# Hedgehog attention beside a Mish FFN on one core: transposes by DMA, the v copy on ScalarE, a new load order and warm-up matmuls

## The chip, the cores and the metric

The kernel runs on one core of a Trainium2 chip. The metric is the device time of one execution in microseconds (us). Below, PE is TensorE (matmuls), PEld its weight loads, DVE is VectorE, ACT is ScalarE, POOL is GpSimd, and SP is SyncE, which here only issues DMA transfers. "Granted clock" is the TensorE clock that the profile reports, as a share of full speed. "Cold" below means that matmuls take as long as the first six v matmuls of the kernel before, 2.29 us (382 ns each), and "warm" that they take as long as its later ones, 1.30 us (217 ns each).

## The reference, cut to what matters

```python
x  = A_x                                  # 1 x 2048 x 448, bf16
xn = layernorm(x)
# linear attention, 16 heads of 28 columns
q, k, v = split_heads(xn @ wqkv)
pq, pk  = q @ w_phi, k @ w_phi            # per head, 28 x 28
phi     = concat(softmax(p), softmax(-p)) # for q and for k
o       = (phi_q @ (phi_k^T v)) / (phi_q @ sum(phi_k) + 1e-6)
# FFN, 448 -> 1792 -> 448, h * tanh(softplus(h)) is Mish
h       = xn @ w1 + b1
out     = x + o @ wo + mish(h) @ w2
```

The kernel multiplies w_phi into the q and k weights first (the products are called Wp), so that one matmul gives pq or pk. For that it transposes the q and k weights; and its matmuls that contract over the 448 columns read xn transposed (the tile xnT).

## The kernel before

Rows are taken in 8 pairs of 128-row tiles; j counts pairs. The operations are recorded by a helper that adds the waits and keeps one list per engine, in the order of the code. One pass of the projection loop, for one pair, is called an iteration; "xT of pair 7" is the transposed xn of pair 7. These are the parts that matter; cuts are marked.

```python
# start-up
dma("SP", x_all[:, 0:2, :], ...)
wload("ACT", Wqkv[:, :, D:2 * D], A_wqkv[:, D:2 * D], "Wk")
dma("SP", x_all[:, 2:4, :], ...)
wload("SP", Wqkv[:, :, 2 * D:3 * D], ..., "Wv")
# ... x 4 to 7, Wq, x 8 to 15, W1, W2, Wo, all on SP
for j in range(4):                         # block-diagonal w_phi
    dma("ACT", Wbd[DH * j:DH * (j + 1), :, DH * j:DH * (j + 1)], ..., r=["Wbd"], w=[f"Wbd{j}"])

def w_trans(which, h):                     # weights transposed on PE, then copied by ACT
    b = 4 + h                              # the banks of the k matmuls
    # ... 8 x e.transpose(PSb[0:KP, b, ...], Wqkv[:, c, col:col + KP], ident[:])
    act(lambda a: a.activation(WT[...], PSb[0:KP, b, :]..., ACT.Copy), ...)

def w_mm(which, h):                        # weights times Wbd, banks 6 and 7, copied by ACT
    # ... 8 matmuls
    act(lambda a: a.activation(Wp[:, which, 2 * h:2 * h + 2, :], PS[:, 6:8, 0:D], ACT.Copy), ...)

def xT(j):                                 # xn transposed on PE, then copied by ACT
    for u in range(2):
        pe(lambda e, t=t, u=u: transp(e, b, xn[t % NXN], u), ...)
    act(lambda a: a.activation(xnT[:, :, 256 * j:256 * j + 256], PSb[:, b, :]..., ACT.Copy), ...)

def vevac(j):                              # v copied out of PSUM by DVE
    dve(lambda v: v.tensor_copy(v_ext[:, 2 * j:2 * j + 2, :, 0:DH], PS[:, 2:4, 0:D]...), ...)

for j in range(NP):                        # the projection loop, NP = 8
    if j + 3 < NP:
        ln_a(j + 3)                        # DVE statistics, POOL rstd
    if j + 1 < NP:
        xT(j + 1)
    if j == 1:
        w_mm(0, 0); w_mm(0, 1)             # q weights
    proj(j, j - 1 if j else None)          # PE: v(j), q(j-1), k(j); vevac(j); q exponentials on ACT
    kexp(j)                                # ACT: two exponentials of k
    if j == 0:
        w_trans(0, 0); w_trans(0, 1)       # q weights
    if j + 2 < NP:
        ln_b(j + 2)                        # DVE: xn of two tiles
    if j >= 2:
        knorm(j - 2)                       # DVE: sum, reciprocal; POOL: product phik
# ... then the FFN with the attention's second half between, and the output
```

The softmax here doesn't subtract the row's maximum and nothing guards it: scores larger than these inputs give would overflow.

## Time and profile before

| | before |
|---|---|
| median of the runs | 186.0 us |
| span of the profiled execution | 184.0 us |
| first v matmul | 12.40 us |
| v matmuls of pair 1 / pair 2 / pair 7 start | 23.11 / 28.11 / 58.01 us |
| last k matmul of the loop ends | 62.55 us |
| first Mish starts | 68.77 us |

From the first Mish on PE is busy for 48.77 of the first 49.20 us, so the table cuts the kernel in three: start-up, loop, FFN. The page of the profile shows the first two in the 40 slices, each 4.6 us long; a digit is the busy share in tenths.

```profile
PE   0775599679879999999999999999999999999993
DVE  1576035989898891148888888300121121121211
ACT  1763749775696884445667666875000000000000
```

PE has its holes in the first five slices, and small ones up to the twelfth. There (slices 8 to 12) DVE is at 8 and 9 while PE is at 6 to 9. An average over the whole span would hide both.

The chain of waits (start, duration, what), followed back from the last instruction, is this in the start-up:

```profile
3.34 5.44 DMA Wbd<-in_A_w_phi_dram
8.91 0.92 PE PS L294 x8
9.85 0.93 ACT Wp L298
...
12.61 2.09 PE PS L309 x6
...
16.46 1.73 ACT hm L358 x2
18.33 0.64 PE PS L284 x8
18.99 1.94 ACT hm L287 x2
20.93 0.91 ACT xnT L321
21.84 0.82 ACT Wp L298
22.70 0.57 PE PS L294 x8
```

Here L294 is the product of weights and w_phi, L298 its copy, L358 the exponentials of k, L284 and L287 the q weight transposes and their copies. Between the k matmuls of pair 0 (16.4 us) and the v matmuls of pair 1 (23.1 us), PE has only 0.64 and 0.57 us of the chain, and ACT nearly all the rest. (PE is busy for 2.49 of these 6.69 us in all; ACT for 5.39.) The transposes of the q weights even wait for the exponentials of k, since they use the same PSUM banks.

The timeline of one iteration of the loop (start, duration, engine, line, operation, output and input, shape, count; in brackets the idle time before it and what ended it):

```profile
46.85 0.70 PE L304 MATMUL PS<-ident,xn 128*128 128x128 bf16 x8 [1.17 <-DVE xn L273]
47.03 2.00 DVE L364 TENSOR_REDUCE Sk<-hm 128x64 f32<-128x1792 bf16 x1
47.39 1.30 PE L309 MATMUL PS<-Wqkv,xnT 128*128 128x448 bf16 x6
...
49.07 0.55 DVE L366 RECIPROCAL rSk<-Sk 128x64 f32<-128x64 f32 x1
49.70 3.21 POOL L367 TENSOR_TENSOR hm<-hm,rSk 128x1792 bf16<-128x1792 bf16 x1 [2.03 <-DVE rSk L366]
...
50.32 1.09 DVE L504 CAST v_ext<-PS 128x896 bf16<-128x896 f32 x1 [0.70 <-PE PS L314]
...
51.33 2.02 DVE L273 TENSOR_SCALAR xn<-x_all,mv,rstd 128x448 bf16<-128x448 bf16 x2
...
53.10 0.70 PE L304 MATMUL PS<-ident,xn 128*128 128x128 bf16 x8 [1.17 <-DVE xn L273]
```

Read it as a ring: PE transposes xn and multiplies; the v copy on DVE waits for PE; xn comes behind the v copy on DVE; PE waits for xn. From 46.85 to 53.10 us the ring takes 6.25 us. The two xn take 2.02 us here, where they start under POOL's product (49.70 to 52.91 us), and 0.69 us where POOL is idle (at 27.13 and 32.05 us). The first of the two takes 1.71 us and ends at 53.04 us, 0.13 us after the product; "held by POOL" below means this.

### The profile page before, as it was taken

The numbers are of one execution on the slowest core, as the hardware profiler recorded it, in microseconds if no ns is written. First come the engines' busy times: TensorE is split into PE (matmuls) and PEld (weight loads), VectorE is DVE, ScalarE is ACT, GpSimd is POOL, SyncE is SP. The second block draws the span as 40 slices with busy tenths as digits, with TensorE's granted clock in tenths as the row PEclk, the third lists the DMA queues.
The fourth block names the chain that finished last, engine by engine and source line by source line (L and its number), as shares of the span: only waits on it lengthen the run. The fifth ranks groups of instructions, "written<-read, shape, count | busy, mean of one in ns | idle before, by whom it ended". The sixth has DMA issues, their size and how long they took to land.

```text
span 184.0 us, 2742 instructions
## 1 busy us (share of the span) xinstructions
PE 164.6 (89%) x1143; PEld 86.5 (47%) x1153; DVE 90.1 (49%) x172; ACT 84.6 (46%) x86; POOL 51.8 (28%) x54
## 2 busy tenths in 40 slices
PE   0775599679879999999999999999999999999993
PEld 0551445334444476645555555434445445445441
DVE  1576035989898891148888888300121121121211
ACT  1763749775696884445667666875000000000000
POOL 4340102395546699104444444200000000000000
PEclk9999999999999999999999999999999999999999
DMA  6999800000000000000000000000001001001001
GB/s 177 349 405 368 258 0 0 0 2 4 0 0 0 2 4 0 4 0 0 4 0 0 4 0 0 0 4 0 25 25 50 28 26 50 27 25 53 25 25 50
DMA packets 7957, 9.15 MB, mean 50 GB/s; under 512 B 1033, under 2 KB 7177, under 8 KB 7945
## 3 DMA queue, kind: packets, MB, share of 16 engines
q1 hardware_dynamic: 6864, 8.49, 13.6%
q10 hardware_dynamic: 1048, 0.48, 0.9%
q8 instruction: 9, 0.15, 0.4%
q14 instruction: 4, 0.02, 0.0%
q0 software_dynamic: 32, 0.00, 0.0%
HBM read 7.14 MB, written 1.84 MB: 49 GB/s over the span
## 4 chain that ended last, share of the span: by engine, by line
PE 81%; DVE 9%; ACT 3%; DMA 3%; issue 1%; ACTq 1%; POOL 0%; POOLq 0%; DVEq 0%
PE PS L309 37%; PE PS L477 23%; PE PS L314 7%; PE PS L410 4%; PE PS L384 4%; PE PS L304 4%; DVE xn L273 3%; DMA Wbd<-in_A_w_phi_dram 3%; DVE v_ext L504 2%; DVE Sk L364 2%; PE PS L294 1%; ACT hm L287 1%; ACT Wp L298 1%; ACT hm L358 1%; ACTq L169 1%
## 5 line engine op out<-in xcount | busy, mean ns | idle before, releaser
L477 PE MATMUL PS<-W,hm 128*128 128x448 bf16 x224 | 43.8, 352 | 0.0
L309 PE MATMUL PS<-xnT,W 128*128 128x512 bf16 x158 | 41.2, 379 | 0.5
L464 ACT ACTIVATE hm<-PS,b1T 128x1024 bf16<-128x1024 f32 x28 | 31.2, 1115 | 20.4 <-PE PS L314 11.6
L488 DVE TENSOR_TENSOR out_sb<-PS,x_all 128x448 bf16<-128x448 f32 x16 | 10.0, 624 | 55.2 <-PE PS L314 33.5
L477 PEld LDWEIGHTS PS<-W,hm 128*128 128x128 bf16 x224 | 21.9, 98 | 20.5
L367 POOL TENSOR_TENSOR hm<-hm,rSk 128x1792 bf16<-128x1792 bf16 x8 | 25.6, 3213 | 14.4 <-DVE rSk L366 9.2
L375 ACT ACTIVATE EqT<-PS 112x1024 bf16<-112x1024 f32 x16 | 15.5, 1021 | 11.9 <-PE PS L314 11.9
L309 PEld LDWEIGHTS PS<-xnT,W 128*128 128x128 bf16 x168 | 14.5, 97 | 11.6 <-issue 1.2
L504 DVE CAST v_ext<-PS 128x896 bf16<-128x896 f32 x8 | 8.7, 1090 | 15.7 <-PE PS L314 15.7
L364 DVE TENSOR_REDUCE Sk<-hm 128x64 f32<-128x1792 bf16 x8 | 16.0, 1995 | 0.0
L358 ACT ACTIVATE hm<-PS 128x896 bf16<-128x896 f32 x16 | 13.8, 925 | 2.8 <-PE PS L309 2.8
L410 PEld LDWEIGHTS PS<-KVZ,EqT 112*128 112x128 bf16 x128 | 9.0, 97 | 9.1 <-DVE t_0 L424 3.0
L309 PE MATMUL PS<-Wqkv,xnT 128*128 128x448 bf16 x48 | 11.6, 378 | 1.5 <-DVE b1T L549 1.5
L427 POOL TENSOR_TENSOR o_sb<-t_0,rden 128x448 bf16<-128x448 f32 x8 | 7.5, 943 | 17.4 <-DVE rden L426 17.4
L410 PE MATMUL PS<-KVZ,EqT 112*128 112x120 bf16 x128 | 12.1, 216 | 0.0
L309 PE MATMUL PS<-Wo,EqT 128*128 128x448 bf16 x48 | 11.8, 354 | 0.0
L309 PE MATMUL PS<-xnT,Wp 128*112 128x512 bf16 x48 | 11.7, 380 | 0.0
L261 DVE BATCH_NORM_STATS2 stats<-x_all 128x6 f32<-128x448 bf16 x16 | 9.1, 610 | 3.8 <-DMA x_all<-in_A_x_dram 3.8
L427 POOL TENSOR_TENSOR o_sb<-t_1,rden 128x448 bf16<-128x448 f32 x8 | 7.5, 942 | 11.1 <-DVE rden L426 11.1
L309 PE MATMUL PS<-Wp,xnT 128*128 128x448 bf16 x48 | 10.5, 354 | 0.0
L273 DVE TENSOR_SCALAR xn<-x_all,mv,rstd 128x448 bf16<-128x448 bf16 x16 | 9.3, 619 | 2.3 <-POOL rstd L269 2.3
L304 PE MATMUL PS<-ident,xn 128*128 128x128 bf16 x64 | 6.2, 244 | 3.6 <-DVE xn L273 3.6
(59 smaller groups left out, 162.3 us busy)
## 6 DMA issues: line engine op xcount, KB each, us to landing
W<-in_B_w_dram SPq DMA_DIRECT2D x2, 896.0 KB, 10.5
out_dram<-out_sb SPq DMA_DIRECT2D x16, 112.0 KB, 1.7
W<-in_B_w_dram SPq DMA_DIRECT2D x1, 1568.0 KB, 15.6
Wqkv<-in_A_wqkv_dram SPq DMA_DIRECT2D x4, 224.0 KB, 5.6
x_all<-in_A_x_dram SPq DMA_DIRECT2D x1, 896.0 KB, 7.9
Wqkv<-in_A_wqkv_dram ACTq DMA_DIRECT2D x2, 224.0 KB, 4.0
x_all<-in_A_x_dram SPq DMA_DIRECT2D x2, 224.0 KB, 3.4
x_all<-in_A_x_dram SPq DMA_DIRECT2D x1, 448.0 KB, 5.9
```

What stands on the lines that cost most here:

```text
L273: eng(lambda v: v.tensor_scalar(xn[t % NXN][:, :], x_all[:, t, :], mv[:, t, 0:1], rstd[:, t:t + 1], op0=ALU.subtract, op1=ALU.mult), r=[f" ...
L304: i = e.transpose(PSb[:, bank, o:o + P], src[:, C0[c]:C0[c] + P], ident[:])
L309: i = e.matmul(out, lhs[:, c, :], rhs[:, c, :], start=(start and n == 0), stop=(stop and n == 2))
L314: return e.matmul(out, lhs[h, 1 + u, :], rhs[h, 1 + u, :], start=start, stop=stop)
L358: act(lambda a, s=s: a.activation(Ek[j % 4][:, :, s, :], PS[:, 4:6, 0:D], ACT.Exp, scale=(1.0 if s == 0 else -1.0)), w=[f"Ek{j % 4}{s}"], ...
L364: dve(lambda v: v.tensor_reduce(Sk[b][:, :], Ek[q][:, :, :, :].rearrange("p t s (h f) -> p (t s h) f", f=DH), AX.X, ALU.add), r=[f"Ek{q}0" ...
L367: pool(lambda g: g.tensor_tensor(phik[:, 2 * j:2 * j + 2, :].rearrange("p t (k f) -> p (t k) f", f=DH), Ek[q][:, :, :, :].rearrange("p t s ...
L375: act(lambda a, s=s: a.activation(EqT[0:KP, s, 2 * gp:2 * gp + 2, tc * 512:(tc + 1) * 512], PS[0:KP, 6:8, :], ACT.Exp, scale=(1.0 if s == ...
L410: i = e.matmul(PS[:, b, g * QG * E2:(g + 1) * QG * E2], EqT[0:KP, s, g, t * P:(t + 1) * P], KVZ[:, s, g, :, :], start=True, stop=True)
L427: pool(lambda g: g.tensor_tensor(o_sb[t % NO][:, :].rearrange("p (h d) -> p h d", d=DH), t1[i][:, :, 0:DH], ap_on(rden[i][:, 0:1], [[1, H] ...
L464: act(lambda a: a.activation(hm[tcp][:, fc, :].rearrange("p (u n) -> p u n", u=2), PS[:, b:b + 2, :], ACT.Mish, bias=b1T[:, fc:fc + 1]), r ...
L477: i = e.matmul(PS[:, bs[u], 0:D], hm[t // 8][:, fc, o:o + P], W2[:, fc, :], start=(u == 0 and fc == 0), stop=(u == 1 and fc == FC - 1))
```

## The change

Its intent: take transposes and their copies off PE and ACT, take the v copy off DVE, shorten the way to Wbd, and have PE at full clock when real work begins.

The new x layout writes xn with its overlapping column chunks already side by side (512 instead of 448 columns), so that one DMA transpose takes a whole pair. The diff, cut to its core (all cuts marked with `# ...`):

```diff
+    def dma_t(eng, out, in_, r=(), w=()):
+        return pr.add(eng, lambda e: e.dma_start_transpose(out, in_), r=r, w=w, dma=True)
-    xnT = sb("xnT", [P, KC, S])
+    xnT = sb("xnT", [P, NT, KC, P])
# ...
-    wload("SP", Wqkv[:, :, 0:D], A_wqkv[:, 0:D], "Wq")
-    dma("SP", x_all[:, 8:16, :], xv[:, 8:16, :], w=[f"x{t}" for t in range(8, 16)])
-    wload("SP", W1[:], B_w1, "W1")
-    dma("SP", W2[:], B_w2.rearrange("(c p) d -> p c d", p=P), w=["W2"])
-    wload("SP", Wo[:], A_wo, "Wo")
+    for g in range(QG):
+        dma_t("SP", WTq[:, g:g + 1, :], A_wqkv[:, g * KP:g * KP + P], w=[f"WTq{g}"])
+    dma("ACT", x_all[:, 8:16, :], xv[:, 8:16, :], w=[f"x{t}" for t in range(8, 16)])
# ... four Wbd loads become one load of w_phi and a masked product on POOL
+    pool(lambda g: g.tensor_tensor(Wbd[:]..., ap_on(wraw[...]), ap_on(mask[...]), ALU.mult), ...)
# ... ln_norm writes 512 columns; w_trans remains for the k weights only
-        act(lambda a: a.activation(Wp[:, which, 2 * h:2 * h + 2, :], PS[:, 6:8, 0:D], ACT.Copy),
-            w=[f"Wp{which}"], x=[6, 7])
+        if eng is act:
+            act(lambda a: a.activation(out, src, ACT.Copy), w=[f"Wp{which}{h}"], x=[bs, bs + 1])
+        else:
+            eng(lambda v: v.tensor_copy(out, src), w=[f"Wp{which}{h}"], x=[bs, bs + 1])
# ...
     def xT(j):
         b = j % 2
+        src = xn[j % NXN]
+        if j >= 2:
+            dma_t("SP", xnT[:, 2 * j:2 * j + 2, :, :].rearrange("p t c n -> p (t c) n"),
+                  src[:].rearrange("p t n -> p (t n)"), r=[...], w=[f"xT{j}"])
+            return
# ... pairs 0 and 1 stay on PE and ACT
     def vevac(j):
-        dve(lambda v: v.tensor_copy(v_ext[:, 2 * j:2 * j + 2, :, 0:DH],
+        act(lambda a: a.activation(v_ext[:, 2 * j:2 * j + 2, :, 0:DH],
# ...
+    pe(lambda e: [e.matmul(PS[:, 7, 0:P], ident[:], ident[:], start=True, stop=True) for _ in range(NWARM)][-1],
+       r=["ident"], x=[7])                 # NWARM = 48, ahead of everything on PE
# ...
     for j in range(NP):
+        if j == 1:
+            w_mm(0, 0, 6, act)
+            w_mm(0, 1, 0, dve)
# ...
         if j + 2 < NP:
             ln_b(j + 2)
+            xT(j + 2)
+            if j < 2:
+                wload("SP", W1[:], B_w1, "W1", (j,))
+            elif j == 4:
+                dma("SP", W2[:], B_w2.rearrange("(c p) d -> p c d", p=P), w=["W2"])
+            elif j == 5:
+                wload("SP", Wo[:], A_wo, "Wo")
```

More of the change, by code (lines that the diff above doesn't have):

```diff
@@ L175, in _kernel @@
     Wbd = sb("Wbd", [KP, QG, KP])
+    wraw = sb("wraw", [KP, QG, DH])
     mask = sb("mask", [KP, QG, E1], FP32)
@@ L179, in _kernel @@
     x_all = sb("x_all", [P, NT, D])
-    xnT = sb("xnT", [P, KC, S])
-    Wqkv = sb("Wqkv", [P, KC, 3 * D])
+    xnT = sb("xnT", [P, NT, KC, P])
+    Wk = sb("Wk", [P, KC, D])
+    Wv = sb("Wv", [P, KC, D])
     Wp = sb("Wp", [P, 2, KC, D])
@@ L189, in _kernel @@
     mhalf = sb("mhalf", [P, 4], FP32)
-    NXN = 6
-    xn = [sb(f"xn{i}", [P, D]) for i in range(NXN)]
+    NXN = 3
+    xn = [sb(f"xn{i}", [P, 2, KC * P]) for i in range(NXN)]
     Sk = [sb(f"Sk{i}", [P, 4 * H], FP32) for i in range(2)]
@@ L200, in _kernel @@
     Ek = [hm0[:, EK0 + i * 4 * D:EK0 + (i + 1) * 4 * D].rearrange("p (t s f) -> p t s f", t=2, s=2) for i in range(4)]
-    WT = hm0[0:KP, 0:2 * KC * QG * P].rearrange("p (w c g n) -> p w c g n", w=2, c=KC, g=QG)
+    WTk = hm0[0:KP, 0:KC * QG * P].rearrange("p (c g n) -> p c g n", c=KC, g=QG)
+    WTq = hm0[:, KC * QG * P:KC * QG * P + QG * D].rearrange("p (g n) -> p g n", g=QG)
     phik = hm[1].rearrange("p a b -> p (a b)").rearrange("p (t f) -> p t f", t=NT)
@@ L218, in _kernel, with wload @@
     FULL = ((0, 2, 3), (0, 1, 3))
-    def wload(eng, dst, src, key):
-        for h in range(2):
+    def wload(eng, dst, src, key, hs=(0, 1)):
+        for h in hs:
             dma(eng, dst[:, 2 * h:2 * h + 2, :],
@@ L228, in _kernel @@
     dma("SP", x_all[:, 0:2, :], xv[:, 0:2, :], w=["x0", "x1"])
-    wload("ACT", Wqkv[:, :, D:2 * D], A_wqkv[:, D:2 * D], "Wk")
+    dma("ACT", wraw[:], bass.AP(tensor=A_w_phi.tensor, offset=A_w_phi.offset, ap=[[DH, KP], [4 * DH * DH, QG], [1, DH]]), w=["wraw"])
+    wload("ACT", Wk[:], A_wqkv[:, D:2 * D], "Wk")
     dma("SP", x_all[:, 2:4, :], xv[:, 2:4, :], w=["x2", "x3"])
-    wload("SP", Wqkv[:, :, 2 * D:3 * D], A_wqkv[:, 2 * D:3 * D], "Wv")
+    wload("SP", Wv[:], A_wqkv[:, 2 * D:3 * D], "Wv")
@@ L239, in _kernel @@
     pool(lambda g: g.memset(ident[:], 0.0), w=["ident"])
-    pool(lambda g: g.memset(Wbd[:], 0.0), w=["Wbd"])
     pool(lambda g: g.memset(mhalf[:], -0.5), w=["mhalf"])
+    pool(lambda g: g.memset(mask[:], 1.0), w=["mask"])
     pool(lambda g: g.affine_select(out=ident[:], in_=ident[:], compare_op=ALU.not_equal, fill=1.0, base=0,
                                    pattern=[[-1, P]], channel_multiplier=1), r=["ident"], w=["ident"])
-    for j in range(4):
-        dma("ACT", Wbd[DH * j:DH * (j + 1), :, DH * j:DH * (j + 1)],
-            A_w_phi.rearrange("(g j) d f -> j d g f", j=4)[j], r=["Wbd"], w=[f"Wbd{j}"])
+    for base, cm, st in ((0, 1, -DH), (DH - 1, -1, DH)):
+        pool(lambda g, base=base, cm=cm, st=st: g.affine_select(
+            out=mask[:], in_=mask[:], compare_op=ALU.is_ge, fill=0.0, base=base,
+            pattern=[[st, QG], [0, E1]], channel_multiplier=cm), r=["mask"], w=["mask"])
@@ L247, in _kernel @@
     dma("POOL", b1_rows[:], B_b1.rearrange("(c p) -> c p", p=P), w=["b1r"])
+    pool(lambda g: g.tensor_tensor(Wbd[:].rearrange("p g (j f) -> p g j f", f=DH),
+                                   ap_on(wraw[:, 0, 0:1], [[DH, QG], [0, QG], [1, DH]]),
+                                   ap_on(mask[:, 0, 0:1], [[0, QG], [E1, QG], [1, DH]]), ALU.mult),
+         r=["wraw", "mask"], w=["Wbd"])
     def masks():
-        pool(lambda g: g.memset(mask[:], 1.0), w=["mask"])
-        for base, cm, st in ((0, 1, -DH), (DH - 1, -1, DH)):
-            pool(lambda g, base=base, cm=cm, st=st: g.affine_select(
-                out=mask[:], in_=mask[:], compare_op=ALU.is_ge, fill=0.0, base=base,
-                pattern=[[st, QG], [0, E1]], channel_multiplier=cm), r=["mask"], w=["mask"])
@@ L272, in ln_norm, with w_trans @@
     def ln_norm(t, eng):
-        eng(lambda v: v.tensor_scalar(xn[t % NXN][:, :], x_all[:, t, :], mv[:, t, 0:1], rstd[:, t:t + 1],
+        i = (t // 2) % NXN
+        eng(lambda v: v.tensor_scalar(xn[i][:, t % 2, :].rearrange("p (a b) -> p a b", a=2),
+                                      ap_on(x_all[:, t, 0:1], [[192, 2], [1, 256]]), mv[:, t, 0:1], rstd[:, t:t + 1],
                                       op0=ALU.subtract, op1=ALU.mult),
-            r=[f"x{t}", f"mv{t}", f"rs{t}"], w=[f"xn{t % NXN}"])
-    def w_trans(which, h):
+            r=[f"x{t}", f"mv{t}", f"rs{t}"], w=[f"xn{i}{t % 2}"])
+    def w_trans(h):
         b = 4 + h
@@ L281, in f, with w_mm @@
                 for g in range(QG):
-                    col = which * D + g * KP
                     o = ((c % 2) * QG + g) * P
-                    i = e.transpose(PSb[0:KP, b, o:o + P], Wqkv[:, c, col:col + KP], ident[:])
+                    i = e.transpose(PSb[0:KP, b, o:o + P], Wk[:, c, g * KP:(g + 1) * KP], ident[:])
             return i
-        pe(f, r=[("Wk" if which else "Wq") + str(h), "ident"], x=[b])
-        act(lambda a: a.activation(WT[:, which, 2 * h:2 * h + 2, :, :], PSb[0:KP, b, :].rearrange(
-            "p (c g n) -> p c g n", c=2, g=QG), ACT.Copy), w=[f"WT{which}{h}"], x=[b])
-    def w_mm(which, h):
+        pe(f, r=[f"Wk{h}", "ident"], x=[b])
+        act(lambda a: a.activation(WTk[:, 2 * h:2 * h + 2, :, :], PSb[0:KP, b, :].rearrange(
+            "p (c g n) -> p c g n", c=2, g=QG), ACT.Copy), w=[f"WTk{h}"], x=[b])
+    def w_mm(which, h, bs, eng):
         def f(e):
@@ L293, in f @@
                 for g in range(QG):
-                    i = e.matmul(PS[:, 6 + c % 2, g * KP:(g + 1) * KP], WT[:, which, c, g, :],
+                    lhs = WTk[:, c, g, :] if which else WTq[0:KP, g, C0[c]:C0[c] + P]
+                    i = e.matmul(PS[:, bs + c % 2, g * KP:(g + 1) * KP], lhs,
                                  Wbd[:, g, :], start=True, stop=True)
             return i
-        pe(f, r=[f"WT{which}{h}"] + [f"Wbd{j}" for j in range(4)], x=[6, 7])
-        act(lambda a: a.activation(Wp[:, which, 2 * h:2 * h + 2, :], PS[:, 6:8, 0:D], ACT.Copy),
-            w=[f"Wp{which}"], x=[6, 7])
+        pe(f, r=([f"WTk{h}"] if which else [f"WTq{g}" for g in range(QG)]) + ["Wbd"], x=[bs, bs + 1])
+        out, src = Wp[:, which, 2 * h:2 * h + 2, :], PS[:, bs:bs + 2, 0:D]
+        if eng is act:
+            act(lambda a: a.activation(out, src, ACT.Copy), w=[f"Wp{which}{h}"], x=[bs, bs + 1])
+        else:
+            eng(lambda v: v.tensor_copy(out, src), w=[f"Wp{which}{h}"], x=[bs, bs + 1])
     def transp(e, bank, src, u):
@@ L305, in transp @@
         return i
+    ALLP = slice(0, P)
     def full(e, out, lhs, rhs, u, start=True, stop=False):
         for n, c in enumerate(FULL[u]):
-            i = e.matmul(out, lhs[:, c, :], rhs[:, c, :], start=(start and n == 0), stop=(stop and n == 2))
+            i = e.matmul(out, lhs(ALLP, c), rhs(ALLP, c), start=(start and n == 0), stop=(stop and n == 2))
         return i
@@ L313, in rem, with f, xs, sl @@
         h = slice(HP * u, HP * (u + 1))
-        return e.matmul(out, lhs[h, 1 + u, :], rhs[h, 1 + u, :], start=start, stop=stop)
+        return e.matmul(out, lhs(h, 1 + u), rhs(h, 1 + u), start=start, stop=stop)
     def xT(j):
         b = j % 2
-        for u in range(2):
-            t = 2 * j + u
-            pe(lambda e, t=t, u=u: transp(e, b, xn[t % NXN], u), r=[f"xn{t % NXN}", "ident"], x=[b])
-        act(lambda a: a.activation(xnT[:, :, 256 * j:256 * j + 256],
-                                   PSb[:, b, :].rearrange("p (c n) -> p c n", c=KC), ACT.Copy),
-            w=[f"xT{j}"], x=[b])
+        src = xn[j % NXN]
+        if j >= 2:
+            dma_t("SP", xnT[:, 2 * j:2 * j + 2, :, :].rearrange("p t c n -> p (t c) n"),
+                  src[:].rearrange("p t n -> p (t n)"), r=[f"xn{j % NXN}{u}" for u in range(2)], w=[f"xT{j}"])
+            return
+        for u in range(2):
+            def f(e, u=u):
+                for c in range(KC):
+                    o = (u * KC + c) * P
+                    i = e.transpose(PSb[:, b, o:o + P], src[:, u, c * P:(c + 1) * P], ident[:])
+                return i
+            pe(f, r=[f"xn{j % NXN}{u}", "ident"], x=[b])
+        act(lambda a: a.activation(xnT[:, 2 * j:2 * j + 2, :, :].rearrange("p t c n -> p (t c n)"),
+                                   PSb[:, b, :], ACT.Copy), w=[f"xT{j}"], x=[b])
+    def xs(t, n):
+        if n == 1:
+            return lambda h, c: xnT[h, t, c, :]
+        return lambda h, c: xnT[h, t:t + n, c, :]
+    def sl(w):
+        return lambda h, c: w[h, c, :]
     def vargs(j, u):
         t = 2 * j + u
-        return PS[:, 2 + u, 0:D], xnT[:, :, t * P:(t + 1) * P], Wqkv[:, :, 2 * D:3 * D]
+        return PS[:, 2 + u, 0:D], xs(t, 1), sl(Wv)
     def kargs(j, u):
         t = 2 * j + u
-        return PS[:, 4 + u, 0:D], xnT[:, :, t * P:(t + 1) * P], Wp[:, 1, :, :]
+        return PS[:, 4 + u, 0:D], xs(t, 1), sl(Wp[:, 1, :, :])
     def qargs(i, u):
@@ L335, in qargs @@
         g = 2 * gp + u
-        return PS[0:KP, 6 + u, :], Wp[:, 0, :, g * KP:(g + 1) * KP], xnT[:, :, tc * 512:(tc + 1) * 512]
+        return PS[0:KP, 6 + u, :], sl(Wp[:, 0, :, g * KP:(g + 1) * KP]), xs(4 * tc, 4)
     def proj(j, i):
@@ L343, in proj @@
                 pe(lambda e, u=u: full(e, *qargs(i, u), u),
-                   r=[f"xT{2 * (i // 2)}", f"xT{2 * (i // 2) + 1}", "Wp0"], x=[6 + u])
+                   r=[f"xT{2 * (i // 2)}", f"xT{2 * (i // 2) + 1}", "Wp00", "Wp01"], x=[6 + u])
         pe(lambda e: (rem(e, *vargs(j, 0), 0), rem(e, *vargs(j, 1), 1))[1], x=[2, 3])
@@ L349, in proj @@
         pe(lambda e: (rem(e, *kargs(j, 0), 0, True, False), rem(e, *kargs(j, 1), 1, True, False))[1],
-           r=["Wp1"], x=[4, 5])
+           r=["Wp10", "Wp11"], x=[4, 5])
         if i is not None:
@@ L353, in proj @@
         for u in range(2):
-            pe(lambda e, u=u: full(e, *kargs(j, u), u, False, True), r=[f"xT{j}", "Wp1"], x=[4 + u])
+            pe(lambda e, u=u: full(e, *kargs(j, u), u, False, True), r=[f"xT{j}", "Wp10", "Wp11"], x=[4 + u])
     def kexp(j):
@@ L440, in fargs @@
         tcp, fc = n // FC, n % FC
-        o = tcp * 1024 + u * 512
-        return PS[:, 2 * (n % 2) + u, :], W1[:, :, fc * P:(fc + 1) * P], xnT[:, :, o:o + 512]
+        return PS[:, 2 * (n % 2) + u, :], sl(W1[:, :, fc * P:(fc + 1) * P]), xs(8 * tcp + 4 * u, 4)
     def ffn1_full(n, u):
@@ L460, in mish @@
         elif fc < 7:
-            rr = [f"WT{w}{h}" for w in range(2) for h in range(2)]
+            rr = ["WTk0", "WTk1"] + [f"WTq{g}" for g in range(QG)]
         else:
@@ L471, in wo @@
             t = 2 * j + u
-            return PS[:, bs[u], 0:D], oT[:, :, t * P:(t + 1) * P], Wo
+            return PS[:, bs[u], 0:D], sl(oT[:, :, t * P:(t + 1) * P]), sl(Wo)
         def f1(e, u):
@@ L492, in _kernel @@
     NP = NT // 2
+    NWARM = 48
     def ln(j, eng):
@@ L503, in vevac @@
     def vevac(j):
-        dve(lambda v: v.tensor_copy(v_ext[:, 2 * j:2 * j + 2, :, 0:DH],
-                                    PS[:, 2:4, 0:D].rearrange("p t (h d) -> p t h d", d=DH)),
+        act(lambda a: a.activation(v_ext[:, 2 * j:2 * j + 2, :, 0:DH],
+                                   PS[:, 2:4, 0:D].rearrange("p t (h d) -> p t h d", d=DH), ACT.Copy),
             w=[f"v{j}"], x=[2, 3])
@@ L517, in ln_b @@
             ln_norm(t, dve)
+    pe(lambda e: [e.matmul(PS[:, 7, 0:P], ident[:], ident[:], start=True, stop=True) for _ in range(NWARM)][-1],
+       r=["ident"], x=[7])
     ln_a(0)
-    w_trans(1, 0)
-    w_trans(1, 1)
+    w_trans(0)
+    w_trans(1)
     ln_b(0)
+    ln_a(1)
     xT(0)
-    ln_a(1)
-    w_mm(1, 0)
-    w_mm(1, 1)
+    w_mm(1, 0, 6, act)
+    w_mm(1, 1, 2, dve)
     ln_b(1)
     ln_a(2)
+    xT(1)
     for j in range(NP):
+        if j == 1:
+            w_mm(0, 0, 6, act)
+            w_mm(0, 1, 0, dve)
         if j + 3 < NP:
             ln_a(j + 3)
-        if j + 1 < NP:
-            xT(j + 1)
-        if j == 1:
-            w_mm(0, 0)
-            w_mm(0, 1)
         proj(j, j - 1 if j else None)
         kexp(j)
-        if j == 0:
-            w_trans(0, 0)
-            w_trans(0, 1)
         if j + 2 < NP:
             ln_b(j + 2)
+            xT(j + 2)
[5 more added lines that the diff above has]
+                wload("SP", Wo[:], A_wo, "Wo")
         if j >= 2:
@@ L552, in _kernel @@
     for u in range(2):
-        pe(lambda e, u=u: full(e, *qargs(7, u), u), r=["xT6", "xT7", "Wp0"], x=[6 + u])
+        pe(lambda e, u=u: full(e, *qargs(7, u), u), r=["xT6", "xT7", "Wp00", "Wp01"], x=[6 + u])
     pe(lambda e: (rem(e, *qargs(7, 0), 0), rem(e, *qargs(7, 1), 1))[1], x=[6, 7])
```

## The prediction

> **What bounds the kernel now.** The span is 184.0 us (timed 186.0). The 40 slices show PE at 7-9 tenths only after the first seventh. Three stages, from the timeline and the table of stretches:
>
> 1. Start-up, 0 to 23 us. The chain of waits shows the four small Wbd loads ending at 8.8 us; then single Wp copies (0.92 us) alternate with cold w_phi products. The first v matmuls (12.4 us) run cold: 382 ns each, against 217 ns later. At 18 to 23 us PE idles again: transposes, copies and products of the q weights, one after another.
> 2. Projection loop, 23 to 62.5 us. Iterations with layer norm take 6.25 us, without it 4.4. The chain alternates PE, v_ext copy on DVE (1.09), xn on DVE, PE. Alone two xn take 0.69 us, but 1.6 to 2.1 while POOL's 3.21 us phik product runs: the first xn ends just when POOL does. [...]
> 3. From the first Mish at 68.8 us to the end, PE is about 99% busy in the FFN. The change leaves this alone.
>
> **What the change does.**
> - Wbd is one load plus a POOL product (estimate 0.95 us, from POOL's 0.94 for 448 columns); ready near 5 us, not 8.8.
> - Warm-up: 48 matmuls from about 2 us, at 130 ns cold, 67 warm, end near 7 us. They delay the k weight transposes by 2.5 us but make what follows warm. First v matmul near 12.9 us, no earlier, but 1 us faster.
> - The q weight transposes (PE) and two WT copies (ACT, 1.94) go; WTq lands in time. PE's 5 us hole becomes about 3. v of j=2: 28.1 before, about 21.5 now.
> - In the loop six pairs' PE transposes (0.6) and ACT copies (1.05) go; the v copy goes from DVE to ACT (estimate 0.92, as the Wp copy). ACT is still 4.6 us per iteration. The cycle q matmuls, v remainder, v copy, two q exponentials gives about 4.9 us instead of 6.25.
> - xn no longer waits for PE, but the DVE-POOL cycle remains: phik 3.21, xn 0.8 (512 columns), reduce 2.0, reciprocal 0.55, about 6.5 us, with a head start. The transposes' landing time is in no trace here; [...] Then xT of pair 7 lands near 47 us, about 1 us late; others just in time.
>
> Sum: last k matmul near 52 us instead of 62.5; ACT then has a backlog, so first Mish near 58.5 instead of 68.8. Saved: about 10 us, nearly all on the critical path; the FFN keeps its length.
>
> **Predicted: 176.0 us**, 80% range 172.5 to 181.0. Faster by over 2%: 0.93; within 2%: 0.05; slower: 0.02.
>
> **What would show it.** PE busy from about 2 us, first v matmul near 13 at 217 ns; loop iterations near 4.9 us with ACT over 90% busy; xn still held to the ends of phik; last phik near 63 (before 74.2); first Mish at 57 to 60; first Mish to end unchanged at 115 us.
>
> **What would make it wrong.** A DMA transpose landing after 6 us or more, or queued behind W1 and W2: v would wait for xT, plus 3 to 6 us. The clock falling cold in gaps after the warm-up: plus 1 to 2. The warm-up ending later than 8 us. FFN matmuls slowing by reading xT in blocks of 128 columns. [...]

The forecast came to 176.0 us, about 10 us saved. The 130 and 67 ns of a warm-up matmul agree with the transposes of the same width in the profile of the kernel before: eight cold ones in 1.03 us (at 6.80 us) and 16 warm ones in 1.07 us (at 18.33 us).

## The result, and the profile after

The median is 174.47 us (173.21 to 175.11, 4 runs). The ratio to the kernel before is 0.9365, with an interval of 0.9309 to 0.9422. A ratio here is the mean time of one kernel's fast runs over that of the other's of the same rounds, so it is not quite the ratio of the medians that are quoted. A second measurement of the same kernel, on another chip, gave 173.60 us and 0.9289 (0.9254 to 0.9324).

| us from the start of the span | before | after | moved by |
|---|---|---|---|
| first v matmul | 12.40 | 11.65 | -0.75 |
| k matmuls of pair 0 end | 16.42 | 16.26 | -0.16 |
| v matmuls of pair 1 start | 23.11 | 16.89 | -6.22 |
| v matmuls of pair 2 start | 28.11 | 22.16 | -5.95 |
| v matmuls of pair 7 start | 58.01 | 45.91 | -12.10 |
| last k matmul of the loop ends | 62.55 | 50.46 | -12.09 |
| first Mish | 68.77 | 56.78 | -11.99 |
| end of the span | 184.0 | 172.1 | -11.9 |

So the gain comes in two halves: 6 us arise between pairs 0 and 1, and 6 us in the loop. After the last k matmul nothing more is won or lost: from the first Mish to the end it is 115.2 us before and 115.3 us after.

The slices after (each 4.3 us):

```profile
PE   6859899999999999999999999999999999999993
DVE  1674966999996003898888883001121112111211
ACT  2374599999989535567766668760000000000000
PEclk9987999999999999999999999999999999999999
```

PE is at 9 from the sixth slice to the last but one. ACT now stands at 8 and 9 through the loop. The last row is news: the granted clock falls in the third and fourth slices.

The chain of waits in the start-up after:

```profile
1.78 5.42 DMA Wk<-in_A_wqkv_dram
7.24 0.67 PE PS L290 x8
7.93 1.03 ACT hm L293
9.01 0.58 PE PS L301 x8
9.62 1.09 DVE Wp L309
...
11.09 0.72 PE PS L339 x8
11.81 2.16 PE PS L321 x6
...
16.30 1.73 ACT hm L386 x2
18.02 0.82 ACT Wp L307
```

The Wbd load has left the chain, but the k weights have taken its place: the second half of them lands at 7.2 us, and a chain of copies follows. That is why the first v matmul is only 0.75 us earlier, although Wbd is now ready at 5.0 us. And the v matmuls (L321, 2.16 us) are as slow as before. The lower end of the chain is short: of the row of q weight steps only one Wp copy is left.

One row of the busy table before (first line: the columns; the clock is the number after the five engines, and the last two are the DMA's):

```profile
core 0: us, PE busy (x) PEld busy (x) DVE busy (x) ACT busy (x) POOL busy (x), PEclk, DMA share, GB/s
12.40:14.80 2.40, 2.40 (x10) 0.88 (x10) 0.30 (x3) 1.27 (x2) 1.07 (x3) 1.00 1.03 405
```

and two rows of the same table after:

```profile
9.60:11.09 1.49, 0.00 (x0) 0.00 (x1) 1.47 (x3) 1.08 (x2) 0.00 (x0) 1.00 1.22 258
...
11.65:14.80 3.15, 3.15 (x14) 0.85 (x12) 2.86 (x10) 1.32 (x2) 1.67 (x4) 0.52 0.13 29
```

PE stands idle from 9.60 to 11.09 us, works for half a microsecond, and then runs at a clock of 0.52 for 3.15 us. So the v matmuls are cold in spite of the warm-up, 2.33 us for six. Before, the same matmuls took 2.29 us for six, as slow as now, while the profile says 1.00: the record holds no clock event before 14.41 us in that run, and the profile counts that as 1.00. The cold state at the start is not in it.

The iteration of the loop after, to be held against the one shown before:

```profile
31.44 1.30 PE L321 MATMUL PS<-Wv,xnT 128*128 128x448 bf16 x6
...
32.79 1.50 PE L321 MATMUL PS<-xnT,Wp 128*112 128x512 bf16 x6
...
33.19 2.62 DVE L279 TENSOR_SCALAR xn<-x_all,mv,rstd 128x512 bf16<-128x512 bf16 x2
...
34.63 0.92 ACT L532 ACTIVATE v_ext<-PS 128x896 bf16<-128x896 f32 x1 [0.28 <-PE PS L326]
...
35.45 1.93 ACT L403 ACTIVATE EqT<-PS 112x1024 bf16<-112x1024 f32 x2
...
36.07 1.30 PE L321 MATMUL PS<-Wv,xnT 128*128 128x448 bf16 x6
...
37.43 1.50 PE L321 MATMUL PS<-xnT,Wp 128*112 128x512 bf16 x6
```

The ring is another one now: q matmuls (32.79), v copy on ACT (34.63, 1.84 us later), two q exponentials (35.45), and the next q matmuls at 37.43, since they need the banks that the exponentials read. That is 4.64 us. PE's own work is not far below: pair 6 to pair 7 of the kernel before, with no transposes and no wait of PE, took 4.37 us (53.64 to 58.01). xn on DVE is in no hurry: it takes 2.62 us, held by POOL, and nobody on PE waits for it, except once: the DMA transpose of pair 7 was issued at 41.81 and landed 4.06 us later, and PE waited 0.4 us for it.

### The profile page after: what moved, and what is told of

It reads as the page before. It is cut to its first block, busy times and chain, and to the rows that moved or that the text cites. A ratio compares the mean times of both kernels' runs of the same rounds, so it can differ in the third digit from the quotient of the medians.

```text
span 172.1 us, 2723 instructions
## 1 busy us (share of the span) xinstructions
PE 163.7 (95%) x1137; PEld 85.0 (49%) x1137; DVE 85.3 (50%) x166; ACT 81.7 (47%) x84; POOL 52.8 (31%) x54
## 3 DMA queue, kind: packets, MB, share of 16 engines
HBM read 6.68 MB, written 1.84 MB: 49 GB/s over the span
## 4 chain that ended last, share of the span: by engine, by line
PE 79%; DVE 9%; DMA 6%; ACT 4%; issue 1%; ACTq 1%; DVEq 0%
PE PS L321 35%; PE PS L504 25%; PE PS L326 7%; PE PS L438 4%; DVE xn L279 4%; PE PS L412 4%; DMA Wk<-in_A_wqkv_dram 3%; DMA xnT<-xn 2%; DVE Sk L392 2%; PE PS L314 2%; DVE stats L266 1%; ACT EqT L403 1%; ACT hm L386 1%; DVE Wp L309 1%; ACT hm L293 1%
## 5 line engine op out<-in xcount | busy, mean ns | idle before, releaser
L321 PE MATMUL PS<-xnT,W 128*128 128x512 bf16 x168 | 43.0, 379 | 0.0
L321 PEld LDWEIGHTS PS<-xnT,W 128*128 128x128 bf16 x168 | 14.5, 97 | 11.6 <-issue 1.2
L321 PE MATMUL PS<-xnT,Wp 128*112 128x512 bf16 x48 | 12.0, 385 | 0.9 <-ACT Wp L307 0.7
L321 PE MATMUL PS<-Wv,xnT 128*128 128x448 bf16 x48 | 11.4, 378 | 0.4 <-DMA xnT<-xn 0.4
L321 PE MATMUL PS<-Wo,EqT 128*128 128x448 bf16 x48 | 11.8, 354 | 0.0
L279 DVE TENSOR_SCALAR xn<-x_all,mv,rstd 128x512 bf16<-128x512 bf16 x16 | 10.8, 718 | 1.2 <-POOL rstd L274 1.2
L321 PE MATMUL PS<-Wp,xnT 128*128 128x448 bf16 x48 | 10.7, 359 | 0.0
L532 ACT ACTIVATE v_ext<-PS 128x896 bf16<-128x896 f32 x8 | 7.4, 919 | 5.5 <-PE PS L326 5.5
L321 PEld LDWEIGHTS PS<-xnT,Wp 128*112 128x112 bf16 x48 | 5.7, 129 | 6.7 <-ACT EqT L403 2.7
```

Of the source, the lines that this page charges most:

```text
L279: eng(lambda v: v.tensor_scalar(xn[i][:, t % 2, :].rearrange("p (a b) -> p a b", a=2), ap_on(x_all[:, t, 0:1], [[192, 2], [1, 256]]), mv[: ...
L321: i = e.matmul(out, lhs(ALLP, c), rhs(ALLP, c), start=(start and n == 0), stop=(stop and n == 2))
```

## The experiments

All times are medians of all timed runs of a label; the ratios use its fast runs alone. A run counts as slow when it is over 1.5% above the fastest of the same kernel: here 333.98 and 181.01 us of e1, 181.05 and 181.52 of e1b, and 184.50 of e4. The fast runs alone have medians of 177.06, 178.78 and 182.10. All kernels gave a correct result. Each run was timed beside the kernel before on the same chip, but not all on one chip; the medians of the kernel before were 186.1 to 187.0 us, so ratios are the safer comparison. e1 to e4 shared a chip, e5 to e7 and e1b another, c0 to c2 a third, and c3 a fourth.

| label | edit | median us | ratio to before (interval) |
|---|---|---|---|
| (the change) | | 174.47 | 0.9365 (0.9309 to 0.9422) |
| c0_after_again | the change, measured again | 173.60 | 0.9289 (0.9254 to 0.9324) |
| e1_v_on_dve | v copy back on DVE | 179.09 | 0.9495 (0.9427 to 0.9562) |
| e1b_v_on_dve | the same kernel again | 180.20 | 0.9568 (0.9523 to 0.9614) |
| e2_x_on_pe | pairs 3 to 7 of xT back on PE and ACT | 176.03 | 0.9441 (0.9372 to 0.9510) |
| e3_both_back | both | 178.93 | 0.9605 (0.9552 to 0.9657) |
| e4_before_v_on_act | before, with the v copy on ACT | 182.38 | 0.9768 (0.9709 to 0.9826) |
| e5_q_on_pe | q weights transposed on PE again | 177.99 | 0.9544 (0.9490 to 0.9597) |
| e6_no_warm | no warm-up matmuls | 174.88 | 0.9347 (0.9312 to 0.9383) |
| e7_filler | 24 more dummy matmuls in the gap | 172.70 | 0.9245 (0.9221 to 0.9270) |
| c1_filler_xn_early | filler, xn ahead of the reciprocal | 172.33 | 0.9215 (0.9183 to 0.9246) |
| c2_reordered | real work in the gap, xn early | 172.07 | 0.9201 (0.9160 to 0.9242) |
| c3_w2_late | the same, W2 loaded later | 171.26 | 0.9151 (0.9111 to 0.9191) |

### The loop: two moves, apart and together

My theory was that the v copy and the x transposes belong to one pair of coupled chains, so that neither move would do much alone and undoing either would bring most of the old loop back. The rival was that the parts simply add up.

e1_v_on_dve undoes the v move:

```diff
-        act(lambda a: a.activation(v_ext[:, 2 * j:2 * j + 2, :, 0:DH], PS[:, 2:4, 0:D]..., ACT.Copy),
+        dve(lambda v: v.tensor_copy(v_ext[:, 2 * j:2 * j + 2, :, 0:DH], PS[:, 2:4, 0:D]...),
```

> The changed kernel with one part undone: the v copy goes back from ScalarE to VectorE. Theory (the loop has two coupled chains): VectorE again carries 1.09 us per pair and PE waits for it, so iterations with layer norm go from 4.63 us back to 6 to 6.5 us, the last k matmul comes about 6 us later and the time is 180 to 183 us. Rival (each part is worth its own work and they add up): the DMA transposes still save their 0.6 us of PE and 1.05 us of ScalarE per pair, so at most half of the loop's 6 us comes back: 176 to 178 us.

Its fast runs took 176.95 and 177.16 us; a third, 181.01, was slow. The profiled run, 333.98 us, was slow too; it is left out of the ratio, though not of the median, and the last section returns to it. So it was run again:

> The same kernel as in the first set with the v copy back on VectorE, run again[...]. With the sum of the parts as the first set showed it: 177 to 178.5 us, and a profile that shows PE waiting for VectorE's v copy in the loop.

It took 178.20 and 179.36 us in the fast runs, and 181.05 and 181.52 in the slow ones: one run was in the range that I gave. The list of waits of that profile (who waited for whom, us in total, times, longest) shows PE waiting in three ways that are absent from the changed kernel, or small there (0.4 us for xnT):

```profile
PE PS L321 <- DMA xnT<-xn: 2.5, 1, 2.5
...
PE PS L321 <- DVE b1T L582: 1.9, 1, 1.9
PE PS L321 <- DVE v_ext L532: 1.8, 2, 1.3
```

The v copy makes PE wait directly; and since it also delays what DVE does after it, the bias copy and the last xn come late too. After the 2.5 us wait the matmuls were slow once more (six v matmuls, at 49.59 us, and six q matmuls, at 51.26 us, took 1.88 and 2.61 us instead of 1.31 and 1.46; the mean granted clock of the run is 0.988), which is part of the time.

e2_x_on_pe keeps the v copy on ACT and takes the x transposes of pairs 3 to 7 back:

```diff
-        if j >= 2:
+        if j == 2:
             dma_t("SP", xnT[:, 2 * j:2 * j + 2, :, :]...)
# ...
         if j + 3 < NP:
             ln_a(j + 3)
+        if 2 <= j and j + 1 < NP:
+            xT(j + 1)
         proj(j, j - 1 if j else None)
# ...
```

> The changed kernel with the transposes of xn pairs 3 to 7 back on PE with a ScalarE copy each (pair 2 stays on DMA), v copy still on ScalarE. Theory (coupled chains): ScalarE then has 4.6 + 1.05 = 5.65 us per iteration and PE again waits for xn, so five iterations grow by 1 to 1.6 us: 179 to 182 us. Rival (parts add up): PE only gets 0.6 us more per pair, five times: about 177.5 us.

e3_both_back makes both edits.

> The changed kernel with both loop parts undone (v copy on VectorE, xn pairs 3 to 7 transposed on PE). Theory: the loop is that of the kernel before, 6.25 us per iteration with layer norm, so 180 to 181 us: start-up alone is worth 5.5 to 6 us, and undoing both costs hardly more than undoing one. Rival (parts add up): the loss is the sum of the two single losses.

e4_before_v_on_act is the kernel before, with nothing but the v copy moved (the first diff of this section, reversed).

> The kernel before with only the v copy moved to ScalarE. Theory (coupled chains): ScalarE then has 5.65 us per iteration and xn still waits for the end of the 3.21 us GpSimd product, so iterations with layer norm go from 6.25 to 5.7 to 6.2 us while those without go from 4.4 to 5.6: 184 to 187 us, no gain over 2%. Rival (parts add up): the move alone brings what its undoing in the first run of this set costs.

The theory with its numbers fell: e2 lost far less than 5 us, and e4 gained about 4 us where I expected nothing (0.9768, with an interval of 0.9709 to 0.9826; whether that is over 2% is unclear). The rival's numbers came closer. But the traces say more than either. This is the mean time of one iteration, from the start of the v matmuls of pair 2 to those of pair 7, divided by five:

| | x transposes on PE | x transposes by DMA |
|---|---|---|
| v copy on DVE | before 5.98, e3 5.86 | e1b 5.81 |
| v copy on ACT | e4 4.98, e2 4.98 | after 4.75 |

The v move is worth 0.9 to 1.1 us per iteration in either column. The DMA transposes are worth 0.23 us with the v copy on ACT, and 0.05 to 0.17 without. So the v move is the main part of the loop's gain (about 5 of 6 us). A rival account is that DVE simply got 1.09 us of work less. The traces speak against it: from one reduction to the next DVE takes 6.24 us before (47.03 to 53.27), and in e4, with the v copy gone from it, still 6.24 and 5.94 us (34.97, 41.21, 47.15), since xn there is held by POOL instead (3.50 us for two in the second of these). What changed is that the v copy was the one place in each iteration where DVE waited for PE. Without it DVE runs ahead, xn is early, and PE does not wait for it. (No run kept the work on DVE and took only the wait away.) In e3, where it is back, the old ring is back with its wait and its 6.3 us:

```profile
39.36 0.72 PE L339 MATMUL PS<-ident,xn 128*128 128x128 bf16 x8 [1.18 <-DVE xn L279]
...
45.63 0.72 PE L339 MATMUL PS<-ident,xn 128*128 128x128 bf16 x8 [1.18 <-DVE xn L279]
```

With the v copy on ACT and the x copies still there, the later iterations of e2 and e4 take 5.1 to 5.2 us. ACT sums to 0.92 for v, 1.93 and 1.74 for the two pairs of exponentials and 1.02 for xT, which is 5.61; at each of the four changes from one of these to the next, ACT starts about 0.1 us before the operation ahead has ended, which leaves about 5.2. In e2 the v copies start 5.10 us apart from 24.93 to 45.33 us, with no idle time of ACT between. So ACT sets the pace there. (Two exponentials of 1.02 us took 1.93 us together, an overlap of the same size.) The DMA transposes take the 1.02 us copy away, and then the ring through PE limits at 4.63 us.

### The start-up: which part brought it

e5_q_on_pe loads the q weights plainly and transposes them on PE after the k exponentials of pair 0, with two ACT copies, as before; the split of the Wp copies over two engines and two bank pairs stays.

```diff
-    for g in range(QG):
-        dma_t("SP", WTq[:, g:g + 1, :], A_wqkv[:, g * KP:g * KP + P], w=[f"WTq{g}"])
+    wload("SP", Wq[:], A_wqkv[:, 0:D], "Wq")
# ...
         kexp(j)
+        if j == 0:
+            w_trans(0, Wq, WTq, "q")
+            w_trans(1, Wq, WTq, "q")
```

> The changed kernel with the q weights loaded plainly and transposed on PE after the first k exponentials, with two ScalarE copies, as before; all else stays. Theory (the start-up gain of 6 us is the q weight path alone, since the end of the first k matmuls moved only from 16.4 to 16.3 us): v of pair 1 starts near 22 to 23 us instead of 16.9, time 179.5 to 181. Rival (warm-up, the one-load Wbd and the copies split over two engines bring a good part): 176 to 178 us.

The hole between the end of the k matmuls of pair 0 and the v matmuls of pair 1 is 6.7 us before (16.42 to 23.11), 5.3 in this run (15.12 to 20.40) and 0.6 after (16.26 to 16.89). So the DMA transposes of the q weights take away 4.7 us of the 6.1, and the rest, 1.4 us, belongs to the other edits there: the copies split over two engines, the second bank pair, and the place of the transposes of pair 2. After the hole the clock had fallen in this run (0.77 from 17 to 19 us): the v and q matmuls of pair 1 took 2.44 and 2.58 us for six, against 1.30 and 1.50 in the changed kernel, and pair 2 started 6.60 us after pair 1, against 5.27.

```profile
20.40 2.44 PE L323 MATMUL PS<-Wv,xnT 128*128 128x448 bf16 x6
22.64 2.58 PE L323 MATMUL PS<-xnT,Wp 128*112 128x512 bf16 x6
```

The time stands about 4 us above the changed kernel (the difference of the ratio to the mean of its two ratios, 0.0217, times 186); that is below the theory's range and at the upper end of the rival's, and pair 1 started at 20.40, not at 22 to 23. The clock is not all of these 4 us: the run of e5 with a mean granted clock of 0.999 took 177.33 us, and those of the changed kernel with 0.999 or more 173.21 to 173.61. So the q weight path is the main part of the start-up's gain, but not the whole of it.

e6_no_warm drops the warm-up:

> The changed kernel without the 48 warm-up matmuls. Theory (the path into the first v matmul runs through the landing of the second half of Wk at 7.2 us and then ScalarE and VectorE copies, not through PE's speed): nothing before 11 us depends on the warm-up by more than 1 us, the first v and k matmuls run cold for certain, time 174.5 to 176. Rival (the prediction: the warm-up makes all of the start-up faster): 176.5 or more.

```diff
-    pe(lambda e: [e.matmul(PS[:, 7, 0:P], ident[:], ident[:], start=True, stop=True) for _ in range(NWARM)][-1],
-       r=["ident"], x=[7])
```

The median is 174.88 us, the ratio lies between the two of the changed kernel. In the profile the first v matmuls took 2.24 us (cold) but the k matmuls after them 1.31 (warm, which I had not expected). The warm-up as the change has it is worth no more than the spread of the runs.

e7_filler adds dummy matmuls where PE stood idle, after the second k weight product:

```diff
     w_mm(1, 1, 2, dve)
+    pe(lambda e: [e.matmul(PS[:, 4, 0:P], ident[:], ident[:], start=True, stop=True) for _ in range(24)][-1],
+       r=["ident"], x=[4])
```

> The changed kernel with 24 more dummy matmuls in PE's idle stretch from 9.6 to 11.1 us. Theory (in the profiled run the clock fell to 0.52 from 11.65 to 14.8 us because PE stood idle just before; in two of the experiments' profiles it did not, so it is a matter of chance in each run): the first v matmuls run at 217 ns in every run, the time sits at the fast end, 172.8 to 173.6, with a smaller spread than the 1.9 us of the changed kernel. Rival (the fall has another cause, such as the light load of the transposes before): same median and spread as the changed kernel, 174.5.

All six runs took 172.46 to 173.14 us (four of them just under the range that I gave), a spread of 0.7 us where the changed kernel had 1.9 and, in its second measurement, 1.0. The repeat of the changed kernel, a yardstick for the last set, also shows whether the fall of the clock is there each time:

> The changed kernel, unaltered, so that the versions of this set can be compared with it on the same chip. 173.2 to 175.2 us, median near 174.5, with the spread of about 2 us that the theory puts down to the clock at the first v matmuls.

It is not. In the profiled run of the repeat the gap is the same, and the clock held. The row of its busy table from 13 to 15 us, columns as above, has a clock of 1.00:

```profile
13.00:15.00 2.00, 2.00 (x14) 0.79 (x13) 1.93 (x7) 1.21 (x2) 1.45 (x4) 1.00 0.03 8
```

and the timeline has its first v matmuls at 1.30 us where the first profile has 2.33:

```profile
12.07 1.30 PE L321 MATMUL PS<-Wv,xnT 128*128 128x448 bf16 x6
```

So in one and the same kernel the clock falls or does not fall, with the same 1.5 us of idling: the length of the gap does not decide it. In the first profile the clock is 1.00 from 8.35 to 11.76 us, 0.50 from 11.76 to 15.17, and 1.00 again from 15.17 to 18.60. It fell in the start-up of two more profiles: 0.55 in e4 (11 to 13 us) and 0.77 in e5 (17 to 19 us). Nor does the busy time of PE in the two microseconds before tell the cases apart:

| profile | PE busy | clock in the 2 us after |
|---|---|---|
| first profile | 0.57 of 9 to 11 us | 0.69 |
| e4 | 0.56 of 9 to 11 us | 0.55 |
| e5 | 0.12 of 15 to 17 us | 0.77 |
| e1b | 0.56 of 9 to 11 us | 1.00 |
| repeat | 0.66 of 9 to 11 us | 1.00 |

What decides was not shown. With the filler, PE was busy for 1.78 of 9 to 11 us in the profile and the clock held. The times go with the mean granted clock for each run: the five runs of the changed kernel with 0.999 or 1.000, on both chips, took 173.21 to 173.61 us, and the five with 0.988 to 0.990 took 173.97 to 175.11. All six runs of the filler have 0.998 or more.

How much the filler gains is less sure: 0.9 us by the medians of the repeat, 1.8 by those of the first measurement, and the chips were not the same.

### Towards a better version

The list of what is left: the gap before the first v matmul, xn held by POOL up to 3.3 us, the late transpose of pair 7, and a loop that ACT and PE set.

c1_filler_xn_early adds to e7 that xn runs on DVE between the reduction and the reciprocal. POOL's product waits for the reciprocal, so xn is meant to start before it:

```diff
     def knorm(j, mid=None):
# ... tensor_reduce
+        if mid:
+            mid()
# ... reciprocal, POOL product
# ...
+        if j >= 2:
+            knorm(j - 2, (lambda: ln_b(j + 2)) if j + 2 < NP else None)
```

> The changed kernel with the 24 filler matmuls, and with each pair's xn placed on VectorE between the reduction and the reciprocal that releases GpSimd's 3.21 us product[...]. Theory (xn waits for the end of the product, up to 3.3 us in the changed kernel, which made pair 7 of xT 0.4 us late): no xn takes over 0.5 us, PE no longer waits for xT, 172.0 to 172.6 us, at most 0.5 us under the version with the filler alone; the loop stays at 4.63 us since ScalarE and PE set it. Rival (the VectorE and GpSimd cycle sets the loop, as half of my prediction had it): 2 us or more faster than the filler version.

Six runs took 172.18 to 172.38 us. Three of the pairs of xn (21.76, 28.97 and 33.20 us) took 0.73 us and ended before the product began. PE no longer waits for xT, and the v matmuls of pairs 4 to 7 start 4.63 us apart to the end. One xn still took 1.65 us: in the iteration without statistics DVE reached it at 36.19 us, before POOL was done (its product ran from 34.48 to 37.69 us), so that expectation was missed. By the medians the gain over the filler alone is 0.4 us (on another chip; the two intervals of the ratio overlap), and the rival's 2 us did not come. So the DVE and POOL cycle does not set the loop; it only stands close behind.

c2_reordered replaces the dummies by real work: the transposes of pair 1 move behind the first v matmuls and the second k weight product gets banks of its own, so that the first v matmul need not wait for either. The v copies of pairs 6 and 7 go to DVE, which has no layer norm left there.

```diff
-    w_mm(1, 1, 2, dve)
+    w_mm(1, 1, 4, dve)
# ...
-    xT(1)
# ... in proj, after the v matmuls
+        if j == 0:
+            xT(1)
# ... in vevac
+        if j >= 6:
+            dve(lambda v: v.tensor_copy(v_ext[:, 2 * j:2 * j + 2, :, 0:DH], ...), ...)
+            return
```

> A version meant to be best: xn early as in the run before; instead of dummy matmuls, the real transposes of pair 1 moved behind the first v matmuls, and the second k weight product into another bank, so that PE has no idle stretch before the first v matmul and starts it near 10.2 us instead of 11.8; the v copies of pairs 6 and 7, where VectorE has no layer norm left, go back to VectorE. Expected 170.5 to 171.8 us: 1 us from the start-up, about 0.5 from the last two iterations. If the clock still falls without the filler, 172 to 173.

It missed its range: 172.07 us. The first v matmul did start at 9.92 us at full clock, and pair 2 was 1.1 us ahead of c1; but the last k matmul ended when it ended in c1, at 48.76 us against 48.74. The chain of waits shows where it went:

```profile
35.14 1.89 DVE xn L279 x2
...
37.05 7.12 DMA xnT<-xn
...
44.21 2.60 PE PS L321 x12
```

The transpose of pair 7 took 7.12 us to land. It stands in the SP queue behind W2, 1568 KB, issued at 34.14 us and landed 9.0 us later. (Whether the order in the queue delays it, or the sharing of the DMA engines, no run separates; the cure is the same.) So the last run loads W2 one pair later, after that transpose:

```diff
-            elif j == 4:
-                dma("SP", W2[:], B_w2.rearrange("(c p) d -> p c d", p=P), w=["W2"])
             elif j == 5:
+                dma("SP", W2[:], B_w2.rearrange("(c p) d -> p c d", p=P), w=["W2"])
                 wload("SP", Wo[:], A_wo, "Wo")
```

> The reordered version with one more edit: W2 is loaded after the transpose of pair 7, not before it. Theory (in the reordered version PE waited 1.2 us for pair 7 of xT because that transpose stood in the same queue behind the 1.57 MB of W2): the transpose of pair 7 lands within 3.5 us of its issue, PE does not wait for xT, and the time is 170.6 to 171.4 us, about 1 us under the reordered version. Rival (pair 7 is late because VectorE and GpSimd finish xn late): the wait of PE for xT stays above 0.7 us and the time at 172.

The DMA part of that profile between 36 and 46 us (operation, size, us from issue to landing) shows W2 and the transpose of pair 7, now ahead of it:

```profile
W<-in_B_w_dram SPq DMA_DIRECT2D x1, 1568.0 KB, 7.4
...
xnT<-xn SPq DMA_TRANSPOSE x1, 3.2
```

3.2 us instead of 7.12, no wait of PE for xT in the whole profile, and 171.26 us (170.85 to 171.57), in the expected range. This is the fastest version: 0.9151 of the kernel before, against 0.9289 for the changed kernel measured again (the intervals lie apart). The chip was another one than for c0 to c2, so the 0.8 us between c2 and c3 are less sure than the wait that is gone. W2 is not needed before the output matmuls, some 70 us later, so its load costs nothing there.

## Why the prediction was right, point by point

The predicted time was 176.0 us and the measured one 174.5, in the range. The split of the kernel in three stages was right, and the third kept its length to 0.1 us.

1. **The start-up, as a whole, right.** Predicted: pair 2 at "28.1 before, about 21.5 now"; measured 22.16. The reason given for the biggest part, "The q weight transposes (PE) and two WT copies (ACT, 1.94) go", is what e5 showed: 4.7 of 6.1 us of the hole. The terms were less right than the sum: of a hole of 5 us the prediction left about 3, and the hole (6.7 us as counted above) shrank to 0.6; the cold matmuls, 1 us, and a wait of 0.7 us for the Wp copy in pair 1 took part of that back. That pair 2 came within 0.7 us was partly luck.
2. **The warm-up, wrong.** "First v matmul near 12.9 us, no earlier, but 1 us faster": it came at 11.65, and in the profiled run it was not faster at all, 2.33 us for six matmuls against 2.29 before. The prediction named the risk ("The clock falling cold in gaps after the warm-up: plus 1 to 2") but did not count on it. e6 showed that the warm-up alone gains nothing that can be told from the spread, and e7 that the runs close up at the fast end once the gap after it is filled. Two errors of about 1 us, of opposite sign, hid each other, which is luck: the first v matmul started 1.25 us earlier than predicted, and its matmuls ran cold. The early start is not the warm-up's end (6.0 us here, not "near 7 us"): the chain runs through the landing of the k weights at 7.2 us, and in the repeat the warm-up ended at 6.9 us and the first v matmul still started at 12.07.
3. **The loop, right in its cause, too small in its size.** The ring "q matmuls, v remainder, v copy, two q exponentials" is the one that the trace shows. The term "about 4.9 us" is the one that was mis-sized: it measured 4.63. The sum of the durations leaves out that ACT starts one operation about 0.1 us before the one ahead ends. From pair 2 to the last k matmul the prediction had 30.5 us (52 less 21.5) and the trace has 28.3 (50.46 less 22.16); of these 2.2 us the shorter ring makes about 1.4 (0.27 times five), and the smaller delay of pair 7 about 0.6.
4. **xn and POOL, right in kind.** xn is still held to the ends of the products, up to 3.3 us, and pair 7 of xT is the one that came late: 0.4 us, not 1. c1, with xn early, came out about 0.4 us faster. The last product ended at 60.3 us, not "near 63".
5. **The DMA transposes: measured, not judged.** The estimate of the landing time is cut from the prediction, since no trace showed it. Measured: the median of the six transposes of xn, 128x1024 each, was 3.6 us, the range 3.0 to 5.8. The risk "queued behind W1 and W2" was real and small in the changed kernel; c2 and c3 showed it at 1.2 us.
6. **The backlog on ACT, as expected in size.** Predicted 6.5 us from the last k matmul to the first Mish, measured 6.3, before 6.2.
7. **What the prediction did not say:** which of the two moves in the loop matters. My later theory, that they work only together, was wrong; the v move alone does most of it.

The difference between the two measurements of the changed kernel (174.47 and 173.60 us) is mainly the clock: it fell, by the mean granted clock, in three of four runs of the first and in two of six of the second. What stays open: how much of the small rest is the chip; and what the 1.4 us of the start-up that are not the q transposes consist of.

## What to carry to other kernels

Look for the instruction through which two engines wait for each other once per iteration, and move that one; in this loop the 1.09 us of work mattered less than that the ring opened, since DVE's own iteration stayed at about 6 us. When you warm the clock up, follow PE to the first real matmul, because after a gap of 1.5 us behind the warm-up the clock was 0.52 for 3.15 us in one profile here and 1.00 in another of the same kernel; with the gap filled all six runs had a mean clock of 0.998 or more. In c2, work moved into the gap (with other edits) replaced the dummies at no loss: 172.07 against 172.33 us. A bulk load that nobody needs soon, issued just ahead of a small transfer that somebody waits for, delayed that transfer here by about 4 us (7.12 against 3.2): issue it behind.

## What else the traces show

- The clock was 0.52 for 3.15 us soon after PE had been idle for 1.49 us (9.60 to 11.09 us), in one profile and not in another of the same kernel, and in e5 it was 0.77 (17 to 19 us) after a gap of 1.91 us.
- The profile can print a clock of 1.00 over slow matmuls. Two cases: the first v matmuls of the kernel before took 382 ns each instead of 217 (the record's first clock event is at 14.41 us), and a run of e1 of 333.98 us has a clock of 1.000 while every output matmul took 581 ns instead of 352. One of the eight executions of that kernel ran so; its cause was not found.
- DMA transposes from issue to landing: SBUF to SBUF, 128x1024 bf16, 3.0 to 5.8 us in the changed kernel, with SP held for 1.23 to 1.27 us (3.81 us behind the load of W2 in c2); from DRAM, 448x128, 4.6 to 8.1 us at start-up beside the other loads.
- With a load of 1568 KB in front in the same queue the transpose of one pair took 7.12 us (c2), with that load behind it 3.2 us (c3).
- Of the 16 xn of the changed kernel two lay under POOL's 3.21 us product and took 2.30 and 3.30 us, one lay beside a POOL memset and a cast and took 0.75, and the other 13 took 0.32 to 0.41.
